# Attention with normalised queries and keys, then a maxout layer: the gains and the softmax scale moved into the queries and keys

## The chip, the cores and the metric

One core of one Trainium2 chip runs the whole program. The metric is the device time of one execution in microseconds (us); for the kernel before, three runs are listed. Beside them stands one execution that the hardware profiler recorded, with every instruction's start and duration.

The engines go by these names in the profile: PE is the matrix engine (PEld its weight loads), DVE the vector engine, ACT the scalar engine, POOL the GpSimd engine, SP the queue that issues most transfers. Each works through its own queue in order and waits for others by semaphores. SBUF is the memory on the chip, PSUM the matrix engine's result memory.

## The reference

Batch 8, 12 heads, 448 positions, head width 64; then 3584 tokens of width 768 through a layer with three weight matrices, their maximum, and an output matrix.

```python
def rmsnorm(x, g):
    rms = np.sqrt(np.mean(x * x, axis=-1, keepdims=True) + 1e-06)
    return x / rms * g
q_n, k_n = (rmsnorm(q, g_q), rmsnorm(k, g_k))
scale = 1.0 / np.sqrt(q.shape[-1])
scores = scale * np.matmul(q_n, k_n.transpose(0, 1, 3, 2))
scores = scores - np.max(scores, axis=-1, keepdims=True)
attn = np.exp(scores)
attn = attn / (np.sum(attn, axis=-1, keepdims=True) + 1e-09)
attn_out = np.matmul(attn, v)
...
h = np.maximum(np.maximum(x @ w1, x @ w2), x @ w3)
return (h @ w_out).astype(np.float32)
```

The gains of queries and keys act on the same 64 columns, so only their product matters to the scores, and the kernel applies it on the query side alone.

## The kernel before

The attention is cut into 48 groups: a batch element and a pair of heads. A group g has four units c, each a quarter of the queries (112 rows) against all keys of both heads. So there are 192 units. The first six groups (`PLAIN`) run in full precision (f32) and are turned by PE; the later ones split each operand into two f16 parts and are turned by transposing transfers on SP.

The order of all work is written out by hand. `beat(g, i)` is called twelve times for each group, three beats for a unit, and puts the steps of several groups next to each other: loads three groups ahead, squares and normalisation two groups ahead, turning one group ahead, scores one unit ahead, the softmax of this unit, the weights' product with the values one group behind. `later(n, work)` queues a step n beats on. Between these steps `thirds` puts matrix products of the maxout layer on PE, for a batch element whose attention is done; the first such products stand in group 6. The weights come as 24 blocks of 64-bit floats, which are decoded by three DVE steps each (`decode`, lines 196, 200 and 205) after one ACT step (`rebias`, line 188), one block every four beats for 18 blocks and one every eight beats for the other six.

The steps that the change and the prediction touch:

- `squares`, `sum_squares` (line 372, DVE) and `inv_rms` (lines 383 and 387, POOL): the sum of squares of each row, and its inverse root by a power of −0.5. `QK_UP` = 2^10 is folded in, so that normalised rows are 1024 times their size.
- `scale_k` and `scale_q` (lines 419, 423 and 394): rows times that root, on POOL, and on DVE for group 0. For groups from 6 on, `scale_q` also multiplies by `gain`, the product g_q g_k divided by its largest magnitude; for earlier groups `keep_whole` does that with `gain_c`, the same values as a column.
- `scores` (lines 545 and 553, PE): into the PSUM tile `sc`, of which there are two, so scores of a unit wait until the unit two back has been read out.
- `row_max` (line 562, DVE): minus the maximum of each row, written to spare columns of `sc`.
- `softmax` (line 570, ACT): `nm`, that maximum times `down`, which undoes 2^20, puts the largest gain back and divides by 8. Then (line 579, ACT) one exponential for each head, with `nm` as bias and `down` as scale, both one value per partition read from memory, and the row's sum as a second output.
- `upper_weights` (lines 648, 652 on DVE, 655 on ACT) and `lower_weights` (line 665, DVE): the weights divided by their sum, as two f16 parts. Line 665 is the last to read `sc`.
- `prep_gain` (lines 875 to 885, DVE): makes `gain`, its largest magnitude and `down` at the start, after the sums of squares of group 0.

Of the kernel before, what the change touches and what calls it, by code (L numbers as in the profile page):

```python
# [9 lines left out]
F32 = mybir.dt.float32  # L10
U32 = mybir.dt.uint32
F16 = mybir.dt.float16
AF = mybir.ActivationFunctionType
ALU = mybir.AluOpType
AX = mybir.AxisListType.X

P = 128
RMS_EPS = 1e-6
# [4 lines left out]

QK_UP = 2.0 ** 10
P_UP = 2.0 ** 15
UP = 2.0 ** 14

# [10 lines left out]
def qknorm_attention_maxout_ffn_kernel(  # L40
# [35 lines left out]
    nc = tc.nc  # L76
    B, H, S, D = q.shape
# [4 lines left out]
    QP = S // NQ  # L82
# [10 lines left out]
    const = ctx.enter_context(tc.tile_pool(name="const", bufs=1))  # L93
    sb = ctx.enter_context(tc.tile_pool(name="sb", bufs=2))
# [38 lines left out]
    nc.scalar.activation(warm, warm, AF.Exp)  # L133
    half_neg = const.tile([P, 15], F32, name="half_neg")
    nc.vector.memset(half_neg, -0.5)

    sums = [const.tile([P, 15], F32, name=f"ss{i}") for i in range(2)]
    for t in sums:
# [30 lines left out]
    def row_largest(dst, src):  # L169
        nc.vector.tensor_reduce(dst, src, axis=AX, op=ALU.max, apply_absolute_value=True)  # L170
# [154 lines left out]
    st = {}  # L325
# [31 lines left out]
    def squares(g, what):  # L357
        s = st[g]
        src = s["kr"] if what == "k" else s["qr"].rearrange("p h c d -> p (h c) d")
        rows, n = src.shape[0], src.shape[1]  # L360
        sq = sb.tile([P, 8, D], F32, name="sq", tag="rows", bufs=3)[:rows, :n]
        if g < 2:
            nc.scalar.activation(sq, src, AF.Square)  # L363
        else:
            nc.gpsimd.tensor_tensor(out=sq, in0=src, in1=src, op=ALU.mult)
        s["sq" + what] = sq
# [3 lines left out]
    def sum_squares(g, what):  # L370
        sq = st[g].pop("sq" + what)
        nc.vector.tensor_reduce(  # L372
            sums[g % 2][:sq.shape[0], KQ[what]], sq, axis=AX, op=ALU.add
        )

    def inv_rms(g, what):
        s, at = st[g], KQ[what]
        if "ri" not in s:
            s["ri"] = sb.tile([P, 15], F32, name="ri", bufs=2).rearrange(
                "p (n o) -> p n o", o=1  # L380
            )
        ri = s["ri"][:, at, 0]
        nc.gpsimd.tensor_scalar(
            out=ri, in0=sums[g % 2][:, at], scalar1=1.0 / D / QK_UP ** 2,
            scalar2=RMS_EPS / QK_UP ** 2, op0=ALU.mult, op1=ALU.add,
        )
        nc.gpsimd.tensor_tensor(out=ri, in0=ri, in1=half_neg[:, at], op=ALU.pow)  # L387

# [23 lines left out]
    def scale_k(g):  # L412
        s = st[g]
        kr, ri = s.pop("kr"), s["ri"]
        kn = key_rows[g % 2]
        on = nc.gpsimd if g else nc.vector
        for h, rows in enumerate(HALVES):
            own = slice(4 * h, 4 * h + 3)
            on.tensor_tensor(
                out=kn[:, h:h + 3, h], in0=kr[:, own],  # L420
                in1=ri[:, own].broadcast_to([P, 3, D]), op=ALU.mult,
            )
            on.tensor_tensor(
                out=kn[rows, 3 - 3 * h, h:h + 1], in0=kr[rows, 3:4],
                in1=ri[rows, 3:4].broadcast_to([64, 1, D]), op=ALU.mult,
            )
        s["kn"] = kn
# [131 lines left out]

    def row_max(g, c):  # L560
        sc = st[g]["sc", c]
        nc.vector.tensor_reduce(  # L562
            sc[:QP, 0, S + 8:S + 10], sc[:QP, :, :S], axis=AX, op=ALU.max, negate=True
        )

    def softmax(g, c):
        s = st[g]
        sc = s["sc", c]
        nm = sb.tile([QP, 2], F32, name="nm", bufs=3)
        nc.scalar.activation(nm, sc[:QP, 0, S + 8:S + 10], AF.Copy, scale=down[:QP])  # L570
        if g < PLAIN:
            if c == 0:
                s["sum"] = sb.tile([QP, NQ, 2], F32, name="sum", bufs=2)
            s["e", c] = sb.tile([QP, 2, S], F32, name="e", tag="pp", bufs=3)
        for h in range(2):
            to, total = sc[:QP, h, :S], sc[:QP, 1, S + 8 + h:S + 9 + h]
            if g < PLAIN:
                to, total = s["e", c][:, h], s["sum"][:, c, h:h + 1]
            nc.scalar.activation(  # L579
                to, sc[:QP, h, :S], AF.Exp, bias=nm[:, h:h + 1], scale=down[:QP],  # L580
                accum_out=total,
            )


# [276 lines left out]
    for i, src in enumerate((g_q, g_k)):  # L861
        nc.scalar.dma_start(
            out=gains[:, i], in_=src.rearrange("(o d) -> o d", o=1).broadcast_to([P, D])
# [4 lines left out]
    load_raw()  # L868
    gain = const.tile([P, D], F32, name="gain")
    g_top = const.tile([P, 2], F32, name="g_top")  # L870
    down = const.tile([P, 1], F32, name="down")
    gain_c = const.tile([P, 1], F32, name="gain_c")

    def prep_gain():
        nc.vector.tensor_tensor(out=gain, in0=gains[:, 0], in1=gains[:, 1], op=ALU.mult)
        row_largest(g_top[:, 0:1], gain)
        nc.vector.tensor_scalar(
            out=g_top[:, 0:1], in0=g_top[:, 0:1], scalar1=LEAST, scalar2=None, op0=ALU.max
        )
        nc.vector.reciprocal(g_top[:, 1:2], g_top[:, 0:1])  # L880
        nc.vector.tensor_scalar(
            out=gain, in0=gain, scalar1=g_top[:, 1:2], scalar2=None, op0=ALU.mult
        )

        nc.vector.tensor_scalar(
            out=down, in0=g_top[:, 0:1], scalar1=1.0 / QK_UP ** 2 / float(D) ** 0.5,
            scalar2=None, op0=ALU.mult,
        )

    for what in "kq":  # L890
        squares(0, what)
    sum_squares(0, "k")
    inv_rms(0, "k")
    sum_squares(0, "q")
    inv_rms(0, "q")
    prep_gain()
    scale_k(0)
    scale_q(0)

# [10 lines left out]
    for what in "kq":  # L910
        squares(1, what)
        sum_squares(1, what)
        inv_rms(1, what)
# [11 lines left out]
    def beat(g, i):  # L925
# [4 lines left out]
        if part == 0:  # L930
            if g < G:
                if k > 4 * PLAIN:
                    row_max(g, c)
                softmax(g, c)
            if early:
                scores(*divmod(k + 1, 4))
            if 0 < k <= 4 * PLAIN:
                turn_plain(*divmod(k - 1, 4))
            elif 0 < k <= 4 * G:
                lower_weights(*divmod(k - 1, 4))  # L940
# [5 lines left out]
        if part == 2:  # L946
            if early:
                row_max(*divmod(k + 1, 4))
            elif k + 1 < 4 * G:
                scores(*divmod(k + 1, 4))  # L950
# [77 lines left out]

    scores(0, 0)
    row_max(0, 0)  # L1030
    for g in range(G + 1):
        for i in range(12):
# [36 lines left out]
```

## Time and profile before

| what | us |
|---|---|
| median of the three runs | 1098.78 |
| lowest and highest | 1097.26, 1098.79 |
| span of the profiled execution, first to last instruction | 1101.6 |
| PE busy in it | 1018.6 |
| ACT busy | 772.1 |
| DVE busy | 757.8 |
| POOL busy | 702.4 |

The profiled execution has no time of its own beside its span, which is 2.8 us above the median of the runs.

A group of instructions is listed by its line, engine, operation, and what it writes and reads (`out<-in`). Busy shares of an engine are averages; the profile also gives them for any stretch of the span, in tenths over 40 slices of 27.5 us each, or as a table. A wait is put down to the instruction that ended last before the waiting one started. The granted clock of PE is given as a share of full speed.

### The profile page before, as it was taken

The page shows a single profiled execution, that of the slowest core. Times are in us where ns is not written, and L with a number is a line of the kernel's source. Part 1 is how long each engine was busy: PE and PEld are TensorE (multiplying, and loading weights), DVE is VectorE, ACT ScalarE, POOL GpSimd, SP SyncE. Part 2 cuts the span into 40 slices and gives each one's busy share as a digit, 9 for nine tenths or more (in the row PEclk, how much of TensorE's full clock was granted, in tenths as well). Part 3 has the DMA queues.
Part 4 walks back from the last instruction along what each step waited for, and adds up shares of the span by engine and source line. Part 5 has one row for each costly group of instructions (what it writes and reads, how often), then busy time and mean ns, then how long its engine had stood idle before and what let it go on. Part 6 is the DMA issues. An engine that isn't in the chain of part 4 may idle for free. (4 is left out here: it accounts for less than half of the span.)

```text
span 1101.6 us, 18390 instructions
## 1 busy us (share of the span) xinstructions
PE 1018.6 (92%) x6168; PEld 501.9 (46%) x6168; DVE 757.8 (69%) x1390; ACT 772.1 (70%) x1767; POOL 702.4 (64%) x805
## 2 busy tenths in 40 slices
PE   4678768988999999999999999999999999999998
PEld 2334333434444455444544454444444454445555
DVE  3899988888667676677677776777677766762210
ACT  4599887767868678687877777778777787773001
POOL 5477988856767767678677686776867677610000
PEclk9687868998989999999999999999999999999999
DMA  5554466856787679877888789787877798563002
GB/s 149 165 164 152 129 180 137 179 115 125 151 166 149 134 151 172 160 148 133 176 155 149 136 169 175 141 151 150 170 146 143 145 166 153 106 106 73 1 1 58
DMA packets 426654, 152.29 MB, mean 138 GB/s; under 512 B 372928, under 2 KB 422336, under 8 KB 426560
## 3 DMA queue, kind: packets, MB, share of 16 engines
q1 hardware_dynamic: 425888, 150.75, 66.8%
q8 instruction: 48, 0.79, 0.3%
q10 hardware_dynamic: 672, 0.38, 0.1%
q14 instruction: 46, 0.38, 0.1%
HBM read 51.97 MB, written 11.01 MB: 57 GB/s over the span
## 5 line engine op out<-in xcount | busy, mean ns | idle before, releaser
L732 PE MATMUL acc<-xt,w_sb 128*128 128x448 f16 x2592 | 520.6, 356 | 0.6 <-ACT m L742 0.6
L732 PEld LDWEIGHTS <-w_sb 128*128 128x128 f16 x2592 | 245.1, 99 | 262.9 <-issue 53.1
L562 DVE TENSOR_REDUCE sc<-sc 112x2 f32<-112x896 f32 x192 | 209.7, 1092 | 47.8 <-PE sc L553 46.6
L579 ACT ACTIVATE sc<-sc,nm,down 112x448 f32<-112x448 f32 x336 | 234.2, 697 | 11.2
L655 ACT ACTIVATE pp<-sc,rs 112x448 f16<-112x448 f32 x336 | 194.8, 632 | 48.5 <-ACT sc L579 40.4
L665 DVE SCALAR_TENSOR_TENSOR pp<-sc,rs,pp 112x448 f16<-112x448 f32 x336 | 212.9, 675 | 3.4 <-ACT pp L655 2.9
L387 POOL TENSOR_TENSOR ri<-ri,half_neg 128x7 f32<-128x7 f32 x96 | 154.2, 1606 | 8.0
L553 PE MATMUL sc<-kt,qt 64*112 64x448 f16 x1008 | 133.7, 371 | 27.1 <-DVE pp L665 23.6
L570 ACT ACTIVATE nm<-sc,down 112x2 f32<-112x2 f32 x192 | 50.7, 264 | 149.5 <-DVE sc L562 148.2
L796 PE MATMUL acc<-wo_sb,ht 128*128 128x384 f16 x864 | 151.4, 330 | 1.4 <-DVE ht L756 0.8
L761 POOL COPY hx<-ht 128x128 f16<-128x128 f16 x48 | 15.5, 323 | 197.7 <-DVE ht L756 191.7
L796 PEld LDWEIGHTS <-ht 128*128 128x128 f16 x864 | 82.0, 99 | 67.5 <-issue 14.5
L703 PE MATMUL av<-pt,vp 128*64 128x448 f16 x1008 | 108.3, 356 | 0.0
L553 PEld LDWEIGHTS <-qt 64*112 64x112 f16 x1008 | 55.0, 128 | 96.9 <-issue 56.4
L648 DVE TENSOR_SCALAR rs<-sc 112x2 f32<-112x2 f32 x168 | 26.6, 158 | 94.7 <-ACT sc L579 94.7
L440 POOL TENSOR_TENSOR kp<-kn,kp 128x512 f16<-128x512 f32 x42 | 50.0, 1190 | 58.9 <-ACT kp L434 58.9
L703 PEld LDWEIGHTS <-vp 128*64 128x64 f16 x1008 | 49.6, 108 | 56.0 <-issue 30.4
L718 DVE SCALAR_TENSOR_TENSOR xt<-av,xt 128x448 f16<-128x448 f32 x42 | 26.2, 625 | 71.1 <-ACT xt L717 71.1
L372 DVE TENSOR_REDUCE ss<-sq 128x7 f32<-128x448 f32 x96 | 60.9, 635 | 10.6 <-ACT sq L363 6.6
L531 POOL TENSOR_TENSOR vp<-vr,vp 128x448 f16<-128x448 f32 x42 | 43.8, 1044 | 32.2 <-ACT vp L525 32.1
L440 POOL TENSOR_TENSOR qp<-qn,qp 112x512 f16<-112x512 f32 x42 | 49.3, 1173 | 21.0 <-ACT qp L434 20.8
L517 POOL TENSOR_SCALAR vr<-vr,v_up 128x448 f32<-128x448 f32 x42 | 60.7, 1446 | 0.0
(112 smaller groups left out, 1203.1 us busy)
## 6 DMA issues: line engine op xcount, KB each, us to landing
raw<-in_moe_w_dram SPq DMA_DIRECT2D x18, 768.0 KB, 4.4
qr<-in_q_dram SPq DMA_DIRECT2D x48, 224.0 KB, 3.0
vr<-in_v_dram SPq DMA_DIRECT2D x96, 96.0 KB, 2.5
kr<-in_k_dram SPq DMA_DIRECT2D x95, 96.0 KB, 3.0
raw<-in_moe_w_out_dram SPq DMA_DIRECT2D x6, 768.0 KB, 5.1
pt<-pp SPq DMA_TRANSPOSE x168, 4.1
out_dram<-osb SPq DMA_DIRECT2D x8, 336.0 KB, 3.2
out_dram<-osb SPq DMA_DIRECT2D x8, 288.0 KB, 3.7
```

The source lines that it names most:

```text
L372: nc.vector.tensor_reduce(sums[g % 2][:sq.shape[0], KQ[what]], sq, axis=AX, op=ALU.add)
L387: nc.gpsimd.tensor_tensor(out=ri, in0=ri, in1=half_neg[:, at], op=ALU.pow)
L440: nc.gpsimd.tensor_tensor(out=parts[:, 1], in0=n, in1=parts[:, 0], op=ALU.subtract)
L517: nc.gpsimd.tensor_scalar(out=vr, in0=vr, scalar1=v_up[:, g // NP:g // NP + 1], scalar2=None, op0=ALU.mult,)
L553: nc.tensor.matmul(sc[:QP, h, :S], qt[rows, qp, c], kt[rows, kp, KEYS[h]], start=n == 0, stop=n == len(TERMS) - 1,)
L562: nc.vector.tensor_reduce(sc[:QP, 0, S + 8:S + 10], sc[:QP, :, :S], axis=AX, op=ALU.max, negate=True)
L579: nc.scalar.activation(to, sc[:QP, h, :S], AF.Exp, bias=nm[:, h:h + 1], scale=down[:QP], accum_out=total,)
L655: nc.scalar.activation(pp[:, 0, h], sc[:QP, h, :S], AF.Copy, scale=rs[:, h:h + 1])
L665: nc.vector.scalar_tensor_tensor(out=pp[:, 1, h], in0=sc[:QP, h, :S], scalar=rs[:, h:h + 1], in1=pp[:, 0, h], op0=ALU.mult, op1=ALU.subtract,)
L703: nc.tensor.matmul(av[half, :S], vp[rows, group, vpart], pt[rows, 7 * wp + group], start=u == 0 and n == 0, stop=u == 3 and n == len(TERMS ...
L732: nc.tensor.matmul(acc[:, :S], wt[:, wp, c], xs[c][:, xp], start=(c == 0 and n == 0), stop=(c == NCT - 1 and n == 2),)
L796: nc.tensor.matmul(acc[:, :HW], lhs, wo_sb[:, f, wp, half * HW:(half + 1) * HW], start=(f == 0 and n == 0), stop=(f == NFT - 1 and n == 2),)
```

## The change

The 2^10 on each side is dropped. Instead keys and queries each carry the root of (largest gain product)/8: for the keys it is folded into the inverse root, since (m·a + e·a)^−0.5 with a = 1/even is the root of `even` times the former value; for the queries it is multiplied into `gain`. The scores then are final, the row maximum is used as it comes, and the exponential's scale is the constant 1.

- `row_max` writes to a tile `nm` of its own (four buffers) instead of spare columns of `sc`; the ACT step of line 570 is gone, and the exponential loses the operand `down`.
- `inv_rms` takes, for keys, two values per partition (`k_mean`, `k_eps`) instead of two constants; for queries the constants change.
- `prep_gain` gets four more DVE steps on one column (`even`, its reciprocal, `k_eps`, `k_mean`), a power of 0.5 of that column on POOL, and a second multiplication of `gain`; the step for `down` is gone. It moves ahead of the sums of squares of group 0, as `inv_rms` needs its results.

```diff
-QK_UP = 2.0 ** 10
+GAIN_MOST = 2.0 ** 24
...
+    half = const.tile([P, 1], F32, name="half")
+    nc.vector.memset(half, 0.5)
...
         ri = s["ri"][:, at, 0]
+        by, eps = 1.0 / D, RMS_EPS
+        if what == "k":
+            by, eps = k_mean, k_eps
         nc.gpsimd.tensor_scalar(
-            out=ri, in0=sums[g % 2][:, at], scalar1=1.0 / D / QK_UP ** 2,
-            scalar2=RMS_EPS / QK_UP ** 2, op0=ALU.mult, op1=ALU.add,
+            out=ri, in0=sums[g % 2][:, at], scalar1=by, scalar2=eps,
+            op0=ALU.mult, op1=ALU.add,
         )
...
     def row_max(g, c):
         sc = st[g]["sc", c]
-        nc.vector.tensor_reduce(
-            sc[:QP, 0, S + 8:S + 10], sc[:QP, :, :S], axis=AX, op=ALU.max, negate=True
-        )
+        nm = sb.tile([QP, 2], F32, name="nm", bufs=4)
+        st[g]["nm", c] = nm
+        nc.vector.tensor_reduce(nm, sc[:QP, :, :S], axis=AX, op=ALU.max, negate=True)
...
-        nm = sb.tile([QP, 2], F32, name="nm", bufs=3)
-        nc.scalar.activation(nm, sc[:QP, 0, S + 8:S + 10], AF.Copy, scale=down[:QP])
+        nm = s.pop(("nm", c))
...
             nc.scalar.activation(
-                to, sc[:QP, h, :S], AF.Exp, bias=nm[:, h:h + 1], scale=down[:QP],
-                accum_out=total,
+                to, sc[:QP, h, :S], AF.Exp, bias=nm[:, h:h + 1], accum_out=total,
             )
...
         nc.vector.reciprocal(g_top[:, 1:2], g_top[:, 0:1])
+        nc.vector.tensor_scalar(
+            out=even, in0=g_top[:, 0:1], scalar1=GAIN_MOST, scalar2=1.0 / float(D) ** 0.5,
+            op0=ALU.min, op1=ALU.mult,
+        )
+        nc.vector.reciprocal(k_mean, even)
+        nc.vector.tensor_scalar(
+            out=k_eps, in0=k_mean, scalar1=RMS_EPS, scalar2=None, op0=ALU.mult
+        )
+        nc.vector.tensor_scalar(
+            out=k_mean, in0=k_mean, scalar1=1.0 / D, scalar2=None, op0=ALU.mult
+        )
         nc.vector.tensor_scalar(
             out=gain, in0=gain, scalar1=g_top[:, 1:2], scalar2=None, op0=ALU.mult
         )
-
+        nc.gpsimd.tensor_tensor(out=even, in0=even, in1=half, op=ALU.pow)
         nc.vector.tensor_scalar(
-            out=down, in0=g_top[:, 0:1], scalar1=1.0 / QK_UP ** 2 / float(D) ** 0.5,
-            scalar2=None, op0=ALU.mult,
+            out=gain, in0=gain, scalar1=even, scalar2=None, op0=ALU.mult
         )
 
     for what in "kq":
         squares(0, what)
+    prep_gain()
     sum_squares(0, "k")
     inv_rms(0, "k")
     sum_squares(0, "q")
     inv_rms(0, "q")
-    prep_gain()
     scale_k(0)
```

More of the change, by code (lines that the diff above doesn't have):

```diff
@@ L870, in qknorm_attention_maxout_ffn_kernel @@
     g_top = const.tile([P, 2], F32, name="g_top")
-    down = const.tile([P, 1], F32, name="down")
+    even = const.tile([P, 1], F32, name="even")
+    k_mean = const.tile([P, 1], F32, name="k_mean")
+    k_eps = const.tile([P, 1], F32, name="k_eps")
     gain_c = const.tile([P, 1], F32, name="gain_c")
```

## The prediction

> **What bounds the kernel now.** I read four views in this order: the page's first two parts, busy time by stretches of the span, the waits of each engine stretch by stretch, and the timeline of the start. The page says which engine could be the bound, and where.
>
> ```profile
> PE 1018.6 (92%) x6168; PEld 501.9 (46%) x6168; DVE 757.8 (69%) x1390; ACT 772.1 (70%) x1767; POOL 702.4 (64%) x805
> PE   4678768988999999999999999999999999999998
> PEclk9687868998989999999999999999999999999999
> ```
>
> PE is the bound from about the tenth slice (275 us) on. Before that it has holes and a lower granted clock. The stretches say who fills the early time (columns: stretch, its length, then busy time and instruction count of PE, PEld, DVE, ACT, POOL; granted clock, DMA share, GB/s).
>
> ```profile
> 20.00:40.00 20.00, 11.25 (x47) 6.02 (x47) 13.26 (x19) 8.95 (x22) 11.46 (x15) 0.69 0.47 131
> 40.00:60.00 20.00, 16.18 (x92) 8.90 (x93) 17.37 (x24) 15.97 (x39) 9.96 (x11) 0.80 0.49 154
> 60.00:80.00 20.00, 15.54 (x91) 7.80 (x90) 18.69 (x27) 18.52 (x41) 12.63 (x12) 0.88 0.59 185
> 80.00:120.00 40.00, 31.80 (x169) 15.99 (x167) 38.67 (x46) 36.02 (x81) 33.69 (x28) 0.80 0.43 137
> 120.00:160.00 40.00, 27.50 (x137) 14.10 (x137) 36.20 (x50) 33.32 (x71) 36.72 (x30) 0.71 0.62 161
> 160.00:200.00 40.00, 34.89 (x176) 15.57 (x176) 34.34 (x57) 32.62 (x67) 32.06 (x31) 0.83 0.70 151
> 200.00:240.00 40.00, 34.63 (x210) 16.00 (x210) 34.64 (x57) 27.45 (x63) 32.20 (x34) 0.96 0.75 156
> 240.00:280.00 40.00, 35.38 (x200) 16.98 (x199) 33.63 (x67) 31.02 (x67) 23.19 (x26) 0.91 0.58 120
> 280.00:320.00 40.00, 36.00 (x226) 17.44 (x226) 27.38 (x55) 31.11 (x75) 31.50 (x38) 0.91 0.83 170
> 320.00:360.00 40.00, 39.83 (x254) 19.06 (x252) 29.19 (x56) 30.41 (x71) 27.14 (x33) 1.00 0.72 140
> 360.00:400.00 40.00, 38.50 (x241) 18.57 (x239) 28.62 (x57) 27.70 (x67) 28.57 (x35) 1.00 0.69 140
> 500.00:600.00 100.00, 99.38 (x631) 48.22 (x632) 71.92 (x142) 75.67 (x178) 72.69 (x89) 1.00 0.84 156
> ```
>
> The reader is to see four stages. Until 40 us no engine is full: a chain of small steps. From 40 to about 146 us (the last full-precision exponential, shown below, starts at 141.3) DVE is 87 to 97% busy and ACT nearly as much, because the weights are decoded there. From 146 to 280 us DVE is still at 84 to 87%, PE at 87 to 88%. From 400 to 1000 us PE is 98 to 99% busy at full clock, and only its last holes can be won.
>
> **The exponential, unit by unit.** A unit is one of the 192 pairs of a group and a quarter of its queries. The change takes out one ACT instruction per unit and one pointer operand from each of its two exponentials.
>
> ```profile
> L570 ACT ACTIVATE nm<-sc,down x192: 238/262/307, 16.7 to 992.7; 112x2 f32<-112x2 f32 x192
> 180.88 0.26 ACT L570 ACTIVATE nm<-sc,down 112x2 f32<-112x2 f32 x1 [0.80 <-DVE sc L562]
> 181.18 0.70 ACT L579 ACTIVATE sc<-sc,nm,down 112x448 f32<-112x448 f32 x1
> L579 ACT ACTIVATE e<-sc,nm,down x48: 712/720/727, 17.0 to 141.3; 112x448 f32<-112x448 f32 x48
> L579 ACT ACTIVATE sc<-sc,nm,down x336: 697/697/699, 146.3 to 993.8; 112x448 f32<-112x448 f32 x168
> L562 DVE TENSOR_REDUCE sc<-sc x192: 1077/1090/1100, 15.6 to 991.6; 112x2 f32<-112x896 f32 x192
> L717 ACT ACTIVATE xt<-av x42: 535/543/545, 196.3 to 1010.6; 128x448 f16<-128x448 f32 x42
> L717 ACT ACTIVATE xt<-av,v_up x6: 627/630/635, 57.6 to 167.7; 128x448 f16<-128x448 f32 x6
> ```
>
> From the start of nm to the start of the first exponential is 181.18 − 180.88 = 0.30 us; this goes from the chain between maximum and exponential. The last two rows are one line at one shape, with a constant as scale and with a pointer: 630 − 543 = 87 ns for the pointer. The exponential keeps its bias pointer, and no row shows a second pointer beside a first. So the saving per exponential lies between 0 and 87 ns; a gain below zero would need the constant to be dearer than the pointer, and these rows exclude it. I take 87, since the pair of rows isolates the operand. A unit then frees 0.30 + 2 × 0.087 = 0.47 us of ACT, 192 × 0.47 = 91 us in all. That is not the gain: ACT is not the bound after 280 us.
>
> The Trainium skill, ScalarE: Activation LUTs, What ACT_TABLE_LOAD costs, says that every [128,1] pointer operand adds about 93 ns to an ACTIVATE, each for itself. By that the unit would free 0.49 us, an estimate, and the sum below would move by 0.5 us; the trace's 87 ns for one pointer agrees, and nothing in it shows two.
>
> The maximum now goes to its own tile in SBUF rather than into spare columns of the scores' PSUM bank. I cost that at nothing: no SBUF-to-PSUM pair of rows for the same reduction exists, the nearest is 1090 ns for this one (line 562 above), and 192 times a few ns hide in DVE's idle time. The tile has four buffers, so its writer waits for an exponential four units back, long over: no new wait.
>
> **The start.** prep_gain moves ahead of the sums of squares on DVE, four small operations and a second multiplication of the gains are added, and a one-column power on POOL.
>
> ```profile
> 4.45 0.62 DVE L372 TENSOR_REDUCE ss<-sq 128x7 f32<-128x448 f32 x1 [3.39 <-ACT sq L363]
> 5.24 0.22 POOL L383 TENSOR_SCALAR ri<-ss 128x7 f32<-128x7 f32 x1 [3.17 <-DVE ss L372]
> 5.54 1.51 POOL L387 TENSOR_TENSOR ri<-ri,half_neg 128x7 f32<-128x7 f32 x1
> 7.04 0.20 POOL L383 TENSOR_SCALAR ri<-ss 128x8 f32<-128x8 f32 x1
> 7.32 1.64 POOL L387 TENSOR_TENSOR ri<-ri,half_neg 128x8 f32<-128x8 f32 x1
> 8.81 0.23 DVE L875 TENSOR_TENSOR gain<-gains 128x64 f32<-128x64 f32 x1 [2.37 <-DMA gains<-in_g_k_dram]
> 9.52 0.17 DVE L880 RECIPROCAL g_top<-g_top 128x1 f32<-128x1 f32 x1
> 9.72 0.26 DVE L881 TENSOR_SCALAR gain<-gain,g_top 128x64 f32<-128x64 f32 x1
> 10.98 0.69 DVE L394 TENSOR_TENSOR qn<-qr,ri 112x512 f32<-112x512 f32 x1
> 20.11 0.81 SPq L342 DMA_DIRECT2D kr<-in_k_dram  x2
> 40.72 0.88 ACT L188 ACTIVATE raw<-raw 128x768 f32<-128x768 f32 x1 [2.96 <-DMA raw<-in_moe_w_dram]
> ```
>
> Today the reciprocal roots are made (5.24 to 8.96) while the gains are still on their way (8.81); that cover goes, because DVE's queue is in order and the sums now stand behind the gains. New order: to 9.72 as now; then even, its reciprocal, k_eps, k_mean at 0.20 each (9.52 to 9.72 is one such step). POOL's power overwrites even, so it also waits for the reciprocal, over at 10.1; with the hand-over of 0.17 (the sum ends at 5.07, POOL starts at 5.24) it starts at 10.3 to 10.45. Its price for one column is not shown: at most 1.51 (seven columns), at least 0.20 (POOL's short operation at 7.04); the eighth column cost 1.64 − 1.51 = 0.13, so I take 1.51 − 6 × 0.13 = 0.73. It ends at 11.2, the second multiplication starts at 11.3, the sum for k at 11.5 and ends at 12.1, POOL's k roots run to 14.1 and its q roots (7.32 − 7.04 = 0.28, then 1.64) to 16.0, and qn runs from 16.1 to 16.8 instead of 10.98 to 11.67. The start is 5.1 us later, between 4.6 and 5.9 for the two prices of the power. Pointer scalars in the k roots (47 more times in the loop) may add some 0.1 us to POOL each; POOL's holes (16.8 of 40 us in 240 to 280) hide it.
>
> Behind that stands everything. The fourth load of keys (20.11) waits for the key buffer of the second group, the values and the third pair of weight blocks queue behind it on SP, and ACT's decode at 40.72 still waits for that transfer. No unit before 42 us has ACT as its limit, so nothing is won there: +5.1 us at 42 us.
>
> **What comes back, stage by stage.** The waits of DVE in 60 to 146, 146 to 280 and 280 to 400 us, then those of PE in 280 to 400 (two rows) and 400 to 1000 (columns: total, times, longest):
>
> ```profile
> DVE xt L718 <- ACT xt L717: 3.7, 3, 1.3
> DVE rs L648 <- ACT sc L579: 8.7, 12, 1.4
> DVE rs L648 <- ACT sc L579: 13.3, 20, 1.4
> PE sc L553 <- ACT sc L579: 2.9, 1, 2.9
> PE sc L553 <- DVE pp L665: 2.8, 4, 1.3
> PE sc L553 <- DVE pp L665: 4.6, 10, 1.3
> ```
>
> 42 to 146: of the 24 units from 17.0 to 141.3 some 20 lie here and free 9.4 us of ACT, but DVE is as full, and it is late next. Its idle time in 40 to 160 is 2.6 + 1.3 + 1.3 + 3.8 = 9.0 us, about 7 of it before 146; so 0 to 7. I take 3, by the 3.7 us that DVE waited for ACT.
> 146 to 280: DVE waited 12 times, 0.73 us each, for the exponential; 12 × 0.47 = 5.6. Bounds 0 (PE late instead) and 8.7. PE idled 4 to 5 us in each 40 there, so it can follow: I take 5.5.
> 280 to 400: PE idled only 4.0 + 0.2 + 1.5 = 5.7 us, the upper bound. It waited five times, and 5 × 0.47 = 2.4: I take 2.5.
> 400 to 1000: at most the 4.6 us of ten waits; half of them are shorter than 0.47, so I take 2.5. After 1000 us there are no exponentials: 0.
> Sum: 3 + 5.5 + 2.5 + 2.5 = 13.5 won, 5.1 lost, 8.4 net. Against the profiled span of 1101.6 that is 1093.2. The median of the runs, 1098.78, lies 2.8 below that span; I carry the difference over and forecast 1090.4 us.
>
> **Rivals.**
> The start decides (slower). Until 280 us DVE, not ACT, sets the pace, so ACT's freed time turns into waits for row maxima, and PE takes the rest. For it: 38.67 of 40 us of DVE. Against it: the 12 waits of 0.73 us. It decides once less than 5.1 − 2.2 = 2.9 us comes back: with 1.5 won in all, 1098.8 + 3.6 = 1102.4.
> The pointer costs nothing beside another. Then a unit frees 0.30 instead of 0.47: 13.5 × 0.30/0.47 = 8.6 won, 3.5 net, 1095.3. For it: no row with two pointers; against it: the 87 ns.
> The clock recovers too. In 160 to 320 us the granted clock is 0.83, 0.96, 0.91, 0.91: (0.17 + 0.04 + 0.09 + 0.09) × 40 = 15.6 us of full-rate time. If shorter PE holes win back half of it at PE's share of 0.88, 6.9 more: 1083.5. Against it: the first holes get 5 us longer.
> The Trainium skill, TensorE: Matmul & The Clock Gate, Part 1, What's actually happening, has the clock follow how busy PE has lately been: throttled by default, released by activity. The trace agrees in that 0.69 to 0.88 stand in the stretches with the most holes and 1.00 where PE is 98% busy.
>
> **How the numbers follow.** Forecast 0.58, within 1085 to 1097; two-pointer rival 0.14; clock rival 0.10; start rival 0.18, a little under half of it short of slower. The range of 1082 to 1100 leaves out the worst of the start rival and the best of the clock rival, some 2 in 10 with the tails. A change of 0.2% (2.2 us) is about what a measurement of this kernel can tell from none. Faster: 0.57 + 0.12 + 0.10 = 0.79, of the forecast, the two-pointer rival and the clock rival; within 0.2%: 0.01 + 0.02 of the first two and 0.08 of the start rival, 0.11; slower: its other 0.10.
>
> **What would show it.** Line 570's 192 instructions are gone, and 192 × 0.262 = 50 us with them; the exponential at 697 becomes 610 ns, and ACT's busy total falls by 50 + 384 × 0.087 = 83 us. The first exponential moves from 17.0 to about 22 us, with the sums of squares behind the gains. DVE's wait for the exponential falls from 8.7 and 13.3 us to a third. A unit in mid-span keeps its length, since PE holds it. The forecast fails if DVE's busy time in 60 to 146 us grows, if the fourth load of keys does not carry the late start on (then it is faster), or if PE's clock falls in 146 to 320 us.

## The result, and the profile after

| | before | changed |
|---|---|---|
| median, us | 1098.26 | 1091.78 |
| lowest to highest, us | 1097.26 to 1098.79 | 1089.37 to 1093.06 |
| span of the profiled execution, us | 1101.6 | 1091.2 |

The ratio is 0.9937, with a 95% interval of 0.992 to 0.9954: 6.5 us faster, where 8.4 was forecast. The two spans lie 10.4 us apart, more than the medians do. The profiled execution of the changed kernel took 1093.06 us for a span of 1091.2, so about 1.9 us lie around a span; by that the profiled execution of before took some 1103.5 (an estimate), about 5 above its median. It was a long one; against e2 below it fell back by 3.4 us, all of it after 146 us. The stages are therefore compared below against an experiment whose profiled execution is typical of its runs.

The page of the changed kernel, its busy times and its granted clock:

```profile
PE 1008.7 (92%) x6168; PEld 497.0 (46%) x6168; DVE 760.4 (70%) x1395; ACT 690.3 (63%) x1575; POOL 714.8 (65%) x806
PEclk9698777999999999999999999999999999999999
```

ACT is 81.8 us lighter (772.1 before; 83 was forecast). That is some twelve times what the kernel gained. The start (timeline; after the start time and the duration come engine, line and operation):

```profile
7.82 0.22 DVE L880 TENSOR_TENSOR gain<-gains 128x64 f32<-128x64 f32 x1 [6.75 <-DMA gains<-in_g_k_dram]
9.09 0.58 POOL L902 TENSOR_TENSOR even<-even,half 128x1 f32<-128x1 f32 x1 [7.01 <-DVE k_mean L892]
9.87 1.21 DVE L374 TENSOR_REDUCE ss<-sq 128x7 f32<-128x448 f32 x2
10.59 0.37 POOL L388 TENSOR_SCALAR ri<-ss,k_mean,k_eps 128x7 f32<-128x7 f32 x1 [0.93 <-DVE ss L374]
13.07 1.76 POOL L392 TENSOR_TENSOR ri<-ri,half_neg 128x8 f32<-128x8 f32 x1
14.86 0.69 DVE L399 TENSOR_TENSOR qn<-qr,ri 112x512 f32<-112x512 f32 x1 [1.28 <-POOL ri L392]
20.41 0.63 ACT L583 ACTIVATE e<-sc,nm 112x448 f32<-112x448 f32 x1 [2.08 <-DVE nm L569]
```

DVE now waits 6.75 us for the gains, and the sums of squares stand behind them, at 9.87 instead of 4.45. qn starts at 14.86 instead of 10.98. The gains happened to land 1.0 us earlier here (7.82) than in the profiled execution of before (8.81), so the shift at equal arrival is 3.88 + 0.99 = 4.9 us.

The stretches in which DVE was full (columns as in the prediction), the stretch from 60 to 146 us of the kernel before and of the changed one, and DVE's waits for the exponential in 146 to 280 and 280 to 400 us:

```profile
60.00:80.00 20.00, 14.98 (x99) 7.76 (x99) 19.86 (x27) 17.52 (x41) 14.75 (x10) 1.00 0.48 156
80.00:120.00 40.00, 30.17 (x168) 14.19 (x166) 39.28 (x46) 32.22 (x69) 33.88 (x27) 0.87 0.43 136
120.00:160.00 40.00, 26.86 (x123) 14.12 (x123) 37.33 (x45) 31.73 (x68) 39.01 (x32) 0.70 0.56 160
```

```profile
60.00:146.00 86.00, 65.44 (x349) 33.25 (x349) 81.34 (x102) 77.67 (x168) 69.99 (x58) 0.79 0.53 160
```

```profile
60.00:146.00 86.00, 63.76 (x355) 31.39 (x353) 83.93 (x101) 71.76 (x157) 73.81 (x57) 0.85 0.49 149
```

```profile
DVE rs L651 <- ACT sc L583: 4.2, 11, 1.4
DVE rs L651 <- ACT sc L583: 4.8, 16, 0.8
```

From 60 to 160 us DVE is busier than before (96.5 of 100 us against 93.6), POOL too (87.6 against 83.0), and only ACT got room (81.5 against 87.9). In 60 to 146 us DVE's busy time went from 81.3 to 83.9 us (it is 81.6 in e2 below, which starts as late); the prediction had named such a growth as a sign of failing. After 146 us DVE's waits for the exponential fell from 8.7 to 4.2 us, about half, and from 13.3 to 4.8, about a third; a third was forecast for both.

### The profile page after: what moved, and what is told of

Read it like the earlier page. It is cut to its first block, busy times and chain, and to the rows that moved or that the text cites. A ratio compares the mean times of both kernels' runs of the same rounds, so it can differ in the third digit from the quotient of the medians.

```text
span 1091.2 us, 18210 instructions
## 1 busy us (share of the span) xinstructions
PE 1008.7 (92%) x6168; PEld 497.0 (46%) x6168; DVE 760.4 (70%) x1395; ACT 690.3 (63%) x1575; POOL 714.8 (65%) x806
## 4 chain that ended last, share of the span: by engine, by line
PE 69%; DVE 4%; ACT 2%; issue 2%; DVEq 0%; ACTq 0%
PE acc L735 37%; PE acc L799 14%; PE sc L558 9%; PE av L706 9%; DVE pp L668 2%; ACT pp L658 1%; DVE nm L569 1%; DVE wo_sb L314 0%; ACT xt L720 0%; ACT wo_sb L309 0%; DVE acc L749 0%; DVE ht L759 0%; DVE v_rows L172 0%; ACT ht L755 0%; ACT kp L439 0%
## 5 line engine op out<-in xcount | busy, mean ns | idle before, releaser
L583 ACT ACTIVATE sc<-sc,nm 112x448 f32<-112x448 f32 x336 | 204.2, 608 | 191.0 <-DVE nm L569 184.4
L569 DVE TENSOR_REDUCE nm<-sc 112x2 f32<-112x896 f32 x192 | 208.2, 1084 | 94.2 <-PE sc L558 92.8
L799 PE MATMUL acc<-wo_sb,ht 128*128 128x384 f16 x864 | 149.2, 326 | 1.1 <-DVE ht L759 0.8
L536 POOL TENSOR_TENSOR vp<-vr,vp 128x448 f16<-128x448 f32 x42 | 43.9, 1045 | 39.0 <-ACT vp L530 38.9
L411 POOL TENSOR_TENSOR qn<-qn,gain 112x512 f32<-112x512 f32 x42 | 54.6, 1299 | 3.3
L399 POOL TENSOR_TENSOR qn<-qr,ri 112x512 f32<-112x512 f32 x47 | 53.6, 1140 | 3.2
```

The source lines that it names most:

```text
L569: nc.vector.tensor_reduce(nm, sc[:QP, :, :S], axis=AX, op=ALU.max, negate=True)
L583: nc.scalar.activation(to, sc[:QP, h, :S], AF.Exp, bias=nm[:, h:h + 1], accum_out=total,)
L799: nc.tensor.matmul(acc[:, :HW], lhs, wo_sb[:, f, wp, half * HW:(half + 1) * HW], start=(f == 0 and n == 0), stop=(f == NFT - 1 and n == 2),)
```

## The experiments

All times are medians of kernels run against the kernel before, each group on one chip, with ratios and 95% intervals to it; before had medians of 1098.2 (e1 to e4), 1098.62 (e5 to e8) and 1098.02 us (e9 and e10). The theory (A) was: a later start of 4 to 5 us, and a return of some 10.5 us that follows from the 0.47 us of ACT freed in each unit.

**Putting back one relief, the other, or both (e1 to e4).** The changed kernel once more:

> The changed kernel itself, on the chip of its three variants. Theory A: the later start costs about 4 us and the shorter ACT work returns about 10.5, so about 6.5 below the kernel before, near 1091.8 us. Rival B (the late start is absorbed by 40 us and the ACT work alone is worth 6.5): the same time; the variants tell the two apart.

It took 1092.23 us, 0.9941 (0.9925 to 0.9956). With both reliefs put back, so that the start and the key roots alone are changed:

```diff
         sc = st[g]["sc", c]
-        nm = sb.tile([QP, 2], F32, name="nm", bufs=4)
-        st[g]["nm", c] = nm
-        nc.vector.tensor_reduce(nm, sc[:QP, :, :S], axis=AX, op=ALU.max, negate=True)
+        nc.vector.tensor_reduce(
+            sc[:QP, 0, S + 8:S + 10], sc[:QP, :, :S], axis=AX, op=ALU.max, negate=True
+        )
...
-        nm = s.pop(("nm", c))
+        nm = sb.tile([QP, 2], F32, name="nm", bufs=3)
+        nc.scalar.activation(nm, sc[:QP, 0, S + 8:S + 10], AF.Copy, scale=ones_c[:QP])
...
-                to, sc[:QP, h, :S], AF.Exp, bias=nm[:, h:h + 1], accum_out=total,
+                to, sc[:QP, h, :S], AF.Exp, bias=nm[:, h:h + 1], scale=ones_c[:QP],
+                accum_out=total,
```

> The changed kernel with the ACT copy of the maximum and the pointer scale of the exponentials put back (the pointer holds 1.0), the maximum in PSUM as before: only the start and the key roots' pointers stay changed. Theory A: about 4 us slower than the kernel before, near 1102 us, first exponential near 20.5 to 21.5 us and the units of 60 to 400 us all late by 3 to 5 us. Rival B: no slower than before, 1098.3, late units having caught up by 146 us.

It took 1103.83 us, 1.0052 (1.0039 to 1.0065): 5.6 us slower than before, for the late start and the pointers in the key roots together. The late start is not absorbed, and rival B falls. The two reliefs together are then worth 1103.83 − 1092.23 = 11.6 us. The copy alone put back (the first two pieces of that diff, so the maximum lies in PSUM again):

> The changed kernel with the ACT copy of the maximum put back (0.30 us in the chain of a unit), the exponential's scale constant. Theory A, the return split by the unit's 0.30 and 0.174 us: 10.5 x 0.30/0.474 = 6.6 us above the changed kernel, near 1098.4. Rival C (only the copy counts): 10.5 above, near 1102.3. Rival D (what counts is the exponentials' length): 1092 to 1093.

1092.88 us, 0.9951 (0.9933 to 0.9969). The pointer alone put back (the last piece):

> The changed kernel with the pointer scale (holding 1.0) put back into both exponentials, 2 x 0.087 us in a unit. Theory A: 10.5 x 0.174/0.474 = 3.9 us above the changed kernel, near 1095.7, the exponential at 697 ns again. Rival C: no change, 1091.8. Rival D: near 1100.

1090.24 us, 0.9926 (0.9913 to 0.9939). A missed with both: 1098.4 and 1095.7 were expected, and neither relief, when it is taken away again alone, costs anything that these intervals show. Shortening two exponentials by a pointer each is worth 10.9 us alone, taking the copy away 13.6 alone, and both 11.6. The returns do not add. The prices themselves were right; groups by line (count, then busy time and mean ns) of e2, e1 and e4:

```profile
L584 ACT ACTIVATE sc<-sc,nm,ones_c 112x448 f32<-112x448 f32 x336 | 234.2, 697 | 11.2
```

```profile
L583 ACT ACTIVATE sc<-sc,nm 112x448 f32<-112x448 f32 x336 | 204.1, 607 | 191.6 <-DVE nm L569 185.1
```

```profile
L583 ACT ACTIVATE sc<-sc,nm,ones_c 112x448 f32<-112x448 f32 x336 | 234.4, 698 | 171.8 <-DVE nm L569 164.7
```

A pointer beside the bias pointer costs 697 − 607 = 90 ns, so the premise of the two-pointer rival is out. The Trainium skill, ScalarE: Activation LUTs, What ACT_TABLE_LOAD costs, has about 93 ns for each pointer operand; the trace agrees, with 90.

Where the 11.6 us arise shows in the first exponential of units 0, 24, 45 and 72; timeline of e2, then of e1, e3 and e4:

```profile
20.57 0.72 ACT L584 ACTIVATE e<-sc,nm,ones_c 112x448 f32<-112x448 f32 x1
150.10 0.70 ACT L584 ACTIVATE sc<-sc,nm,ones_c 112x448 f32<-112x448 f32 x1
278.82 0.70 ACT L584 ACTIVATE sc<-sc,nm,ones_c 112x448 f32<-112x448 f32 x1
410.68 0.70 ACT L584 ACTIVATE sc<-sc,nm,ones_c 112x448 f32<-112x448 f32 x1
```

```profile
20.38 0.63 ACT L583 ACTIVATE e<-sc,nm 112x448 f32<-112x448 f32 x1 [2.08 <-DVE nm L569]
149.66 0.60 ACT L583 ACTIVATE sc<-sc,nm 112x448 f32<-112x448 f32 x1
272.97 0.61 ACT L583 ACTIVATE sc<-sc,nm 112x448 f32<-112x448 f32 x1 [1.59 <-DVE nm L569]
401.72 0.61 ACT L583 ACTIVATE sc<-sc,nm 112x448 f32<-112x448 f32 x1 [0.30 <-DVE nm L569]
```

```profile
20.55 0.63 ACT L584 ACTIVATE e<-sc,nm 112x448 f32<-112x448 f32 x1
147.45 0.61 ACT L584 ACTIVATE sc<-sc,nm 112x448 f32<-112x448 f32 x1
270.70 0.61 ACT L584 ACTIVATE sc<-sc,nm 112x448 f32<-112x448 f32 x1
399.77 0.61 ACT L584 ACTIVATE sc<-sc,nm 112x448 f32<-112x448 f32 x1
```

```profile
20.43 0.72 ACT L583 ACTIVATE e<-sc,nm,ones_c 112x448 f32<-112x448 f32 x1 [2.08 <-DVE nm L569]
146.50 0.69 ACT L583 ACTIVATE sc<-sc,nm,ones_c 112x448 f32<-112x448 f32 x1
269.15 0.70 ACT L583 ACTIVATE sc<-sc,nm,ones_c 112x448 f32<-112x448 f32 x1 [1.63 <-DVE nm L569]
399.67 0.70 ACT L583 ACTIVATE sc<-sc,nm,ones_c 112x448 f32<-112x448 f32 x1 [0.29 <-DVE nm L569]
```

The lengths in us that follow (the last row goes to the end of the span: 1101.9, 1090.5, 1089.0 and 1088.5):

| units | e2, no relief | e1, both | e3, pointer gone | e4, copy gone |
|---|---|---|---|---|
| 0 to 24 | 129.53 | 129.28 | 126.90 | 126.07 |
| 24 to 45 | 128.72 | 123.31 | 123.25 | 122.65 |
| 45 to 72 | 131.86 | 128.75 | 129.07 | 130.52 |
| 72 to the end | 691.2 | 688.8 | 689.2 | 688.8 |

So e1 won 0.25, 5.4, 3.1 and 2.4 us in the four stages. The earlier profiled execution of the changed kernel, which is the same program, agrees: 129.24, 124.06, 128.79 and 688.7. In the first stage either relief alone won 2.6 to 3.5 us where both together won almost nothing. What differs there is DVE's own work: its three decode steps of the first 18 blocks took 58.8 us in e2, 58.7 in e3 and 59.9 in e4, but 61.5 in e1 and 62.9 in the earlier execution. These are one or two executions of each kernel, and that of e3 lies 2.0 us below the median of its runs; that the longer decode is what took the gain back is likely and not shown. Against it stands e6 below, where the decode took 60.0 us and the first 24 units still 128.5.

Why the second relief adds nothing late shows in the waits of 400 to 1000 us, of e2, of e3 and of e1:

```profile
DVE rs L653 <- ACT sc L584: 72.6, 108, 1.2
DVE sc L567 <- PE sc L558: 37.2, 29, 2.2
PE sc L558 <- DVE pp L670: 4.1, 10, 1.3
```

```profile
DVE sc L567 <- PE sc L558: 54.8, 45, 2.6
DVE rs L652 <- ACT sc L584: 49.9, 88, 0.8
PE sc L558 <- DVE pp L669: 2.1, 2, 1.1
```

```profile
DVE nm L569 <- PE sc L558: 78.6, 53, 2.9
DVE rs L651 <- ACT sc L583: 22.6, 88, 0.5
PE sc L558 <- DVE pp L668: 1.9, 2, 1.0
```

DVE's wait for the exponential goes 72.6, 49.9, 22.6 us; its wait for PE's scores goes 37.2, 54.8, 78.6. In e4 the two are 38.9 and 64.4. Most of what ACT gives, DVE hands on as waiting for PE. PE's own waits for DVE fall from ten to two with the first relief, whichever it is, and stay there. Why the second relief adds nothing in units 24 to 45 either is not shown.

**The gains on one side (e5).** The whole g_q g_k / 8 goes into `gain`, the key roots have constants, and group 0 is normalised, and its turning issued, before the gains are needed (that last part is not in this cut):

```diff
     def prep_gain():
-        nc.vector.tensor_tensor(out=gain, in0=gains[:, 0], in1=gains[:, 1], op=ALU.mult)
-        ...
+        nc.vector.scalar_tensor_tensor(
+            out=gain, in0=gains[:, 0], scalar=1.0 / float(D) ** 0.5, in1=gains[:, 1],
+            op0=ALU.mult, op1=ALU.mult,
+        )
...
-    prep_gain()
     sum_squares(0, "k")
...
     scale_q(0)
+    prep_gain()
```

> The changed kernel with the whole product g_q g_k / 8 on the query side: no root, no pointers in the key roots, and the gains needed only after group 0 is normalised (the bound on very large gains and the even split are left out). Theory A: the first exponential at 15.5 to 17.5 us instead of 20.4, so the start's 4 us come back and possibly 1 more: 1086 to 1088 us. Rival B (the start is absorbed): 1091 to 1092.

1087.32 us, 0.9899 (0.9883 to 0.9915); its first exponential starts at 15.68 us, 4.7 before e1's, and by the two ratios 4.6 us come back, give or take 2.4. The time comes back by about as much as the start moves. The pointers in the key roots are gone here too; e6 asks for their part.

**Constants in the key roots after group 0 (e6).**

```diff
-        if what == "k":
+        if what == "k" and g == 0:
             by, eps = k_mean, k_eps
```

> The changed kernel with constants in the key roots after group 0, so those keys do not carry the root (scores of these groups come out scaled otherwise). The pointers cost POOL 0.16 us in each of 47 instructions. Theory A (hidden in POOL's holes): within 1 us of the changed kernel, 1091 to 1092. Rival E (POOL is on the path between 80 and 160 us): 2 to 4 us faster, 1088 to 1090.

1090.73 us, 0.9935 (0.992 to 0.995). The pointers do cost POOL 160 ns an instruction (272 ns before, 432 after, on average). The time lies between what A and E expected, and its interval overlaps that of e1, so whether they cost the kernel anything stays open between nothing and some 3 us.

**A lighter DVE, before and after (e7, e8).**

```diff
-        for stage in range(3):
+        for stage in (0, 2):
             later(2 + stage, lambda stage=stage: decode(raw, f, stage), True)
```

> The kernel before with the second of three decode steps left out (the weights lose their signs): 24 DVE instructions of about 1.2 us, 28 us of DVE between 18 and 280 us. If DVE sets the pace there (theory A): 15 to 25 us faster than before, 1073 to 1083. If ACT sets it: 0 to 5 us faster.

> The changed kernel with the same decode step left out. Theory A: with DVE lighter, ACT is the limit for longer, so the change is worth more than its 6.5 us between these two kernels: 9 to 13 us below the lightened kernel before, with the stretch from 42 to 146 us shortened by 3 to 5 us more. Rival (the change's gain does not depend on DVE): 6.5 below it.

1089.68 us, 0.992 (0.9907 to 0.9933), and 1076.03 us, 0.9802 (0.9784 to 0.982). The lightened kernel before fell between the two expectations, 8.9 us faster, for some 28 us less work on DVE. Between the lightened pair the change is worth 13.7 us instead of 6.5, more than the 9 to 13 that A expected; the rival's 6.5 is out. The first exponentials of units 0 and 24 (timelines of e7, then e8):

```profile
16.20 0.72 ACT L579 ACTIVATE e<-sc,nm,down 112x448 f32<-112x448 f32 x1
142.20 0.70 ACT L579 ACTIVATE sc<-sc,nm,down 112x448 f32<-112x448 f32 x1
```

```profile
20.82 0.63 ACT L583 ACTIVATE e<-sc,nm 112x448 f32<-112x448 f32 x1 [2.08 <-DVE nm L569]
141.06 0.60 ACT L583 ACTIVATE sc<-sc,nm 112x448 f32<-112x448 f32 x1
```

These 24 units take 126.0 and 120.2 us: 5.8 won by the lighter ACT where the full decode let through 0.25. With the full ACT work the lighter decode wins 3.3 (126.0 against the 129.3 of the kernel before), and with both reliefs 9.1 (120.2 against the 129.28 of e1). So in the changed kernel DVE is the cap of these units, and in the kernel before both engines hold them. The profiled execution of e8 lies 3.5 us above the median of its runs, so its stages are rather long.

**POOL's squares on ACT (e9), and that with e5 (e10).**

```diff
-        if g < 2:
+        if g < 12:
             nc.scalar.activation(sq, src, AF.Square)
```

> The changed kernel with the squares of groups 2 to 11 on ACT instead of POOL: some 2.0 us a group off POOL, some 1.2 us a group onto ACT. Theory F (with ACT lighter, DVE sets the pace up to 280 us, and its decode is stretched by POOL instructions beside it): DVE's 54 decode steps of the first 18 blocks fall from 61 to 63 us to 58 or less, and the kernel is 2 to 5 us faster than the changed one, 1087 to 1090. Rival G (ACT's time is the limit in 42 to 146 us as it was): the 10 x 1.2 us of ACT come out 2 to 6 us slower, 1094 to 1098.

> The kernel with the whole gain on the query side and the squares of groups 2 to 11 on ACT. If the two are worth what each is alone: theory F 1083 to 1085 us; rival G 1089 to 1093, the other one being worth 5 us.

e9 took 1088.3 us, 0.9907 (0.9888 to 0.9925), by the ratios 3.7 below e1, and e10 1082.95 us, 0.9856 (0.9835 to 0.9878), the fastest of all and 15 us below the kernel before. Both figures of theory F came, in e9's time and in the 54 decode steps, which fell to 57.8 us where 58 or less was expected; ACT had room for the squares. The two larger decode steps of the first 18 blocks on DVE, in e1 and then in e9:

```profile
L207 DVE SCALAR_TENSOR_TENSOR w_sb<-raw,w_sb 128x768 uint32<-128x768 uint32 x18 | 26.9, 1494 | 0.2
L202 DVE SCALAR_TENSOR_TENSOR w_sb<-raw,w_sb 128x768 uint32<-128x768 uint32 x18 | 22.6, 1253 | 0.2
```

```profile
L207 DVE SCALAR_TENSOR_TENSOR w_sb<-raw,w_sb 128x768 uint32<-128x768 uint32 x18 | 24.3, 1349 | 0.2
L202 DVE SCALAR_TENSOR_TENSOR w_sb<-raw,w_sb 128x768 uint32<-128x768 uint32 x18 | 20.9, 1162 | 0.2
```

Same instructions on the same data, 4.3 us shorter with less of POOL beside them, and the first 24 units of e9 take 125.86 us where e1 takes 129.28. One execution each: the size is rough, and a lighter POOL may help by itself too.

## Why the prediction was right, point by point

- The start, forecast at 5.1 us: right. It is 4.9 in the trace at equal arrival of the gains; e2 measured 5.6 (4.3 to 7.1) in the runs and e5 got 4.6 back, both with the key roots' pointers in the figure. In the steps, the one-column power took 0.58 us (0.73 taken, between 0.20 and 1.51), and the key root's first step 0.37 where 0.22 had stood. The fourth load of keys carried the late start on, as forecast: it started at 24.08 instead of 20.11, and ACT's decode at 44.71 instead of 40.72. e2 and e5 show that the late start is not absorbed.
- 0.47 us of ACT a unit: right; the exponential went from 697 to 607 ns. The maximum's new place, put at nothing, made that reduction 8 ns shorter (1092 to 1084 ns), 1.5 us of DVE in all.
- Units 0 to 24, forecast at 3 us: the term that was mis-sized. It gave 0.25 between e2 and e1. The term took DVE's idle time as free to be won and DVE's own work as fixed. With one relief that held (e3 won 2.6, e4 3.5); with both, DVE's decode of the first 18 blocks took 61.5 and 62.9 us instead of 58.8 (59.7 in the kernel before). The prediction had named the growth of DVE's busy time in 60 to 146 us as a sign of failing; it came, and it points at this term. That the decode grows under POOL's instructions, e9 supports; why both reliefs bring it about and one does not stays open.
- 146 to 280, forecast at 5.5: 5.4 (units 24 to 45). 280 to 400, forecast at 2.5: 3.1 (units 45 to 72). 400 to the end, forecast at 2.5: 2.4. The sizes are right, and in part by luck. The first two were counted as waits times the relief for each, which takes return and relief to be proportional, and e3 and e4 show that they are not: by 12 waits, a relief of 0.18 us (e3) would win 2.2 in units 24 to 45 and one of 0.30 (e4) 3.6, and they won 5.5 and 6.1. The bounds, what DVE or PE waited in all, were the sound part.
- So 11.2 (stages) to 11.6 (runs) came back instead of 13.5, and 5.6 went instead of 5.1. By e1 and e2 the net is about 6 us, by the first runs 6.5, not 8.4.
- Two small readings were off without consequence: PE idled 4.6 to 5.4 us in each 40 us from 146 to 280, not 4 to 5, and the dearer pointer that it weighs against its 87 ns would move the sum by some 0.2 us (12 ns for each of 17 counted waits), not 0.5.
- The two-pointer rival, had its premise been true, would still not have cost 4.9 us, since e4 pays for the pointers and is as fast.
- The clock rival did not come: the granted clock of e1, 0.962 over the span, and of e2, 0.964, are alike. In 160 to 320 us e2 has 0.91, 0.96, 0.96 and 0.96 without any relief, so the lower clock in the trace of before was not ACT's doing. The rival by which the start decides was half right: its start is there, and DVE holds the first 24 units of the changed kernel, but not the later ones.
- That POOL's holes hide the pointers: open (e6).

## What to carry to other kernels

A shared preparation that moves ahead of the first work costs its full wait, because the first group has nothing in front of it; a value needed later should be asked for later, as e5 does. When several engines are near full, the first relief of one can return nearly all that there is to win and the second nothing, as here: read who waits next (here DVE, then PE), and move work onto the freed engine, as e9 and e10 do. Put each part of a change back alone; a sum of waits times relief can be right in total and wrong in its parts. Before comparing stages of two traces, check by the runs whether each profiled execution is a typical one.

## What the runs showed of the hardware that was not expected

A DVE instruction with two SBUF inputs can be stretched fourfold by POOL instructions beside it. Timeline of the changed kernel; line 207 takes 0.95 us in the median:

```profile
84.73 4.18 DVE L207 SCALAR_TENSOR_TENSOR w_sb<-raw,w_sb 128x768 uint32<-128x768 uint32 x1
85.57 0.93 POOL L367 TENSOR_TENSOR sq<-kr 128x448 f32<-128x448 f32 x1
86.46 1.64 POOL L274 TENSOR_TENSOR w_sb<-w_sb 128x768 f16<-128x768 f32 x1
88.06 1.75 POOL L367 TENSOR_TENSOR sq<-qr 112x512 f32<-112x512 f32 x1
```

Three POOL instructions, each with two inputs, start while DVE's one lasts, and the page of the profile counts all of it as busy. Of the 18 such DVE instructions in this trace, the eight with no two-input POOL instruction beside them took 0.94 to 0.96 us, and five beside a narrow one (64 columns) or a power took 0.93 to 0.95; the other five, beside POOL instructions of 448 to 768 columns, took 1.27 to 4.41. The Trainium skill, GPSIMD Engine Reference, Specifications, says that the two engines share SBUF interfaces and contend when a DVE instruction has two SBUF inputs; the trace agrees, with 4.18 against 0.95 us. And on POOL, two pointer scalars on a 128 by 7 instruction cost 160 ns, beside a median of 212 ns for one with constants.
